# Windowed attention feeding a two-layer FFN: 128-token units for the first groups, a staged fp32 first block, 64-row score matmuls, and DMA transposes from the second batch on

## The chip, the core and the metric

One core of one Trainium2 chip runs the whole program. The metric is device time in microseconds (us), the median of several executions; fast executions of one kernel agree here within about 1%. A profile is one of these executions, recorded by the hardware. Its span runs from the first to the last instruction; it is some 2 us shorter than the time of the run.

## The reference

There are 8 batches, 8 heads, 576 tokens and a head size of 64. Attention looks back over at most 128 tokens, with a linear bias per head. Its output, read as 4608 tokens of 512 features, goes through two matrix products with a squared ReLU between them.

```python
scores = q @ k.T / 8                          # per batch and head, 576 x 576
rel    = pos[:, None] - pos[None, :]
scores = where((rel >= 0) & (rel < 128), scores - slope[h] * abs(rel), -1e9)
x      = softmax(scores) @ v                  # then 4608 tokens x 512
out    = relu(x @ w_in) ** 2 @ w_out          # w_in 512 x 2048, w_out 2048 x 512
```

All inputs and the output are fp32 in device memory.

## The kernel before

A small planner in Python lists every piece of work with an estimated duration, simulates the engines, and emits the instructions of each engine in the order that came out. On the chip each engine then as a rule takes its list in that order. If the next item's data is not there, the engine waits, even if a later item could run.

Attention is cut into 40 blocks of up to 128 tokens: five per batch, 128, 128, 128, 128 and 64 tokens. Blocks are numbered here from 0 through all batches, so block 5 is the first of the second batch. The FFN is cut into nine groups of 512 tokens. The pieces that matter:

```python
# loads: all by GpSimd's software queue, fp32 -> bf16 on the way
nc.gpsimd.dma_start(o, src[b, :, kb*128:kb*128+n, :].rearrange("h s d -> s h d"))   # k, q, v of one block
# order of loads: blocks 0-4, w_in (4 quarters), blocks 5-9, w_out (4 quarters), the rest

# per block: q and k transposed on TensorE (8 per block), copied out; q into tiles half zero
nc.tensor.transpose(slot.tile[:, i*128:(i+1)*128], src[:, (i % C)*128:(i % C + 1)*128], ident)

# scores of two heads at once: 128 rows, the zeros of qp keep the heads apart, 2n columns
nc.tensor.matmul(ps[:, :, part, 0:n], kT[...][:, c, :], qp[...][:, c, :, 0:n], start=True, stop=True)
...                                            # exp (ScalarE), mask (VectorE), P @ v, normalise
nc.tensor.transpose(xp[:, c*128:(c+1)*128], xt[...][:, c*128:(c+1)*128], ident)     # 4 per block

# FFN, group g: 16 steps of 4 matmuls with 512 columns (h), then 16 parts of 4 matmuls (o)
nc.tensor.matmul(h, w_in_sb[:, cc, fc*128:(fc+1)*128], xT[:, cc, g*512:(g+1)*512], ...)
nc.tensor.matmul(o, g_tile[:, fc, t*128:(t+1)*128], w_out_sb[:, fc, :], ...)
```

Group 0 cannot start before all of blocks 0 to 3 are in `xT`.

The softmax here doesn't subtract the row's maximum and nothing guards it: scores larger than these inputs give would overflow.

Of the kernel before, what the change touches and what calls it, by code (L numbers as in the profile page):

```python
# [14 lines left out]
class Task:  # L15


    __slots__ = ("engs", "key", "emit", "deps", "acq", "rel", "nout", "users",
                 "ready", "start", "end", "eng", "seq", "lat", "dma")

    def __init__(self, engs, key, emit, deps=(), acq=(), rel=(), lat=None, dma=None):

        self.engs, self.key, self.emit = engs, key, emit
        self.deps = [d for d in deps if d is not None]
        self.acq, self.rel, self.lat = list(acq), list(rel), lat
        self.dma = dma
        self.users, self.ready, self.start, self.end = [], 0.0, None, None
# [9 lines left out]
class Plan:  # L37


    LAT = {"PE": 260.0, "ACT": 220.0, "DVE": 220.0, "POOL": 200.0, "SP": 2200.0}  # L40
    BEGIN = {"POOL": 1250.0}
# [14 lines left out]
    def order(self):  # L56
        used = {tag: [] for tag in self.bufs}
        free = {}
        cand = {}
        left = {}  # L60
        for t in self.tasks:
            left[t] = len(t.deps)
            for d in t.deps:
                d.users.append(t)
            for e in t.engs:
                free.setdefault(e, self.BEGIN.get(e, 800.0))
                cand.setdefault(e, [])
# [5 lines left out]
        def avail(t):  # L73
            at = t.ready
            for s in t.acq:
                u = used[s.tag]
                n = self.bufs[s.tag]
                if len(u) >= n:
                    old = u[len(u) - n]
                    if old.left:  # L80
                        return None
                    at = max(at, old.freed)
            return at
# [3 lines left out]
        while len(done) < n_all:  # L87
            best = None
            for e, c in cand.items():
                lo = None  # L90
                for t in c:
                    a = avail(t)
                    if a is None:
                        continue
                    st = max(a, free[e])
                    k = (st, t.key, t.seq)
                    if lo is None or k < lo[0]:
                        lo = (k, t)
                if lo is not None and (best is None or lo[0][0] < best[0]):
                    best = (lo[0][0], e, lo[1])  # L100
            if best is None:
                raise RuntimeError("plan is stuck: " + repr([
                    (e, t.key, [s.tag for s in t.acq if avail(t) is None]) for e, c in cand.items() for t in c
                    if e != "POOL"][:40]))
            st, e, t = best
            t.eng, t.start = e, st
            dur = t.engs[e]
            if t.dma is not None:
                at = max(st + dur + 900.0, self.dma_free)
                self.dma_free = at + t.dma  # L110
                t.end = self.dma_free + 900.0
# [23 lines left out]
def kernel(  # L135
# [16 lines left out]
    NBLK = B * NKB  # L152

# [7 lines left out]
    far = const.tile([128, 2, 128], FP32)  # L161
    w_in_sb = const.tile([128, C, d_ff], BF16)
# [3 lines left out]
    def ring(name, n, shape):  # L166
        return [const.tile(shape, BF16, name=f"{name}_{i}") for i in range(n)]



    size = {"kn": 4, "qn": 4, "v": 6, "kT": 4, "qp": 3, "P": 3, "x": 2}
    kn = ring("kn", size["kn"], [128, d_model])
    qn = ring("qn", size["qn"], [128, d_model])
    vt = ring("vt", size["v"], [128, H, D + 1])
    kT = ring("kT", size["kT"], [128, C, 128])
    qp = ring("qp", size["qp"], [128, C, 2, 128])
    Pt = ring("P", size["P"], [128, H, 2, 128])
    xt = ring("x", size["x"], [128, d_model])

    plan = Plan({"h": 2, "o": 2, "s": 2, "att": 2, "rec": 4, "rt": 3, "g": 2, "osb": 3, **size})  # L180

    def act(n):
        return n * 0.84 + 55.0
# [3 lines left out]

    def mm(n):
        return max(n, 64) / 2.4 + 1.5



# [4 lines left out]
    t_iota = plan.add({"POOL": 360.0}, -9e5 + 0.012, build_iota)  # L197
# [4 lines left out]
    t_ident = plan.add({"DVE": 230.0}, -9e5 - 1, build_ident, [t_iota])  # L202
# [8 lines left out]
    t_dist = plan.add({"DVE": 1300.0}, -9e5 + 0.5, build_dist, [t_ident])  # L211
    t_mask = []

    for h in range(H):
        def build_mask(h=h):
            nc.scalar.activation(masks[:, h], dist, AF.Exp, bias=0.0,  # L216
                                 scale=-(2.0 ** (-8.0 * (h + 1) / H)))
        t_mask.append(plan.add({"ACT": act(256)}, -9e5 + h, build_mask, [t_dist]))

    def zero():  # L220
        for t in qp:
            nc.vector.memset(t[0:64, :, 1, :], 0.0)
            nc.vector.memset(t[64:128, :, 0, :], 0.0)
    t_zero = plan.add({"DVE": 2000.0}, -9e5, zero)

    def ones():
        for t in vt:
            nc.vector.memset(t[:, :, D:D + 1], 1.0)
        for t in vt[NKB - 1:]:
            nc.vector.memset(t[64:128, :, 0:D], 0.0)  # L230
    t_ones = plan.add({"DVE": 1200.0}, -9e5 + 1, ones)


    def load(key, ns, emit, deps=(), acq=()):
        return plan.add({"POOL": 900.0}, key, emit, deps, acq, dma=ns)
# [4 lines left out]
    def load_w_in(key):  # L240
        for n in range(4):
            def emit(n=n):
                w = d_ff // 4
                nc.gpsimd.dma_start(
                    w_in_sb[:, :, n * w:(n + 1) * w],
                    moe_w_in[:, n * w:(n + 1) * w].rearrange("(c p) f -> p c f", p=128))
            t_win[n] = load(key + n, 2550.0, emit)

    def load_w_out(key):
        for n in range(4):  # L250
            def emit(n=n):
                nc.gpsimd.dma_start(
                    w_out_sb[:, 4 * n:4 * n + 4, :],
                    moe_w_out[n * 512:(n + 1) * 512, :].rearrange("(c p) f -> p c f", p=128))
            t_wout[n] = load(key + n, 2550.0, emit)

    s_in, t_in = {}, {}

    def load_block(m, key):
        b, kb = divmod(m, NKB)  # L260
        n = blk[kb]
        for i, (nm, dst, src, tag) in enumerate((("k", kn, k, "kn"), ("q", qn, q, "qn"), ("v", vt, v, "v"))):
            sl = s_in[m, nm] = Slot(tag)

            def emit(dst=dst, src=src, sl=sl, nm=nm):
                o = dst[sl.idx]
                o = o[0:n, :, 0:D] if nm == "v" else o[0:n].rearrange("s (h d) -> s h d", h=H)
                nc.gpsimd.dma_start(o, src[b, :, kb * 128:kb * 128 + n, :].rearrange("h s d -> s h d"))  # L268
            t_in[m, nm] = load(key + 0.01 * i, 1050.0 * n / 128, emit, [t_ones] if nm == "v" else [], [sl])

    for m in range(NKB):
        load_block(m, -9e5 + m)
    load_w_in(-8e5)
    for m in range(NKB, 2 * NKB):
        load_block(m, -7e5 + m)
    load_w_out(-6e5)
    for m in range(2 * NKB, NBLK):
        load_block(m, -5e5 + m)


    t_xT = {}
    chain = {"tp": [], "s": [], "pv": [], "xp": []}

    def copy(task, o, i):
        if task.eng == "DVE":
            nc.vector.tensor_copy(o, i)  # L286
        else:
            nc.scalar.activation(o, i, AF.Copy)  # L288

    def attention(m):  # L290
        b, kb = divmod(m, NKB)
        n = blk[kb]
        due = (b * S + kb * 128 + n) / 4 - 192 - 150
        first = b == 0


        sk, sq = Slot("kT"), Slot("qp")
        sk_of[m] = sk
        slot = Slot("h" if first else "att")
        last = None  # L300
        for i in range(2 * C):
            def emit(i=i):
                nm = "kq"[i // C]
                src = (kn if i < C else qn)[s_in[m, nm].idx]
                if i == 0:
                    slot.tile = psum.tile([128, 1024], BF16, tag=slot.tag, name="tp")
                nc.tensor.transpose(slot.tile[:, i * 128:(i + 1) * 128], src[:, (i % C) * 128:(i % C + 1) * 128],  # L307
                                    ident)
            last = plan.add({"PE": mm(128)}, due - 56, emit,
                            [last, t_ident, t_in[m, "kq"[i // C]]] + ([t_in[m, "q"]] + chain["tp"] if i == 0 else []),  # L310
                            [slot, sk, sq] if i == 0 else [], [s_in[m, "kq"[i // C]]] if i % C == C - 1 else [])
        chain["tp"] = [last]

        def evac_k():
            copy(t_k, kT[sk.idx][:, :, 0:n], slot.tile[:, 0:512].rearrange("p (c s) -> p c s", c=C)[:, :, 0:n])
        both = {"ACT": act(C * n), "DVE": dve(C * n, 2)}
        t_k = plan.add(both if first else {"DVE": both["DVE"]}, due - 56, evac_k, [last], [], [slot])
        t_q = []
        for c2 in range(2):
            def evac_q(c2=c2):  # L320
                po = c2 * 64
                o = qp[sq.idx][po:po + 64, :, c2, 0:n]
# [182 lines left out]
    key = 0  # L505
# [46 lines left out]
```

## Time and profile before

The time before is 350.76 us (4 runs, 350.66 to 350.84). The page of the profile, its first two parts (busy us and share of the span; then busy tenths in 40 slices of 8.7 us):

```profile
span 349.0 us, 6481 instructions
PE 329.7 (94%) x2451; PEld 186.9 (54%) x2496; DVE 198.2 (57%) x600; ACT 203.2 (58%) x392; POOL 107.3 (31%) x133
PE   2689999999999999999999999999999999999995
DMA  9999999999999579595796867760000100110021
```

TensorE (PE) is busy almost throughout, and the DMA row stands at 9 for the first 113 us; I call that "full". (The row adds up the times of packets, which overlap, so that the sum per engine can come to more than 1.) "Busy" is pipelined time: neighbouring matmuls overlap, so it does not tell what a matmul costs. For that, read the starts. Lines of the timeline of TensorE around 145 us (start, duration, operation, count):

```profile
143.14 0.19 PE L382 MATMUL pv<-vt_83,P_94 128*128 128x65 bf16 x1
143.17 0.20 PE L382 MATMUL pv<-vt_84,P_94 128*128 128x65 bf16 x1
145.14 0.39 PE L307 MATMUL tp<-ident,kn_72 128*128 128x128 bf16 x4
145.37 0.39 PE L307 MATMUL tp<-ident,qn_76 128*128 128x128 bf16 x4
145.59 1.03 PE L483 MATMUL o<-w_out_sb,g 128*128 128x512 bf16 x3
```

The P·V matmul of 65 columns lasts 0.19 us, but the next starts 0.03 us later. Eight transposes go by in 0.45 us, so one costs 56 ns. In the same way 512 columns cost 215.7 ns and 256 columns 109 ns. Multiplying by the counts gives the table below. I call the rest of the span *lost time*: the time up to some moment, less the start-to-start cost of the matmuls begun by then. (Some h and o matmul records are missing from the traces, so these two kinds were counted by their weight loads, which are complete.)

| TensorE work before | count | us |
|---|---|---|
| h and o, 512 columns | 1152 | 248.5 |
| scores, 256 or 128 columns | 224 + 64 | 28.0 |
| P·V, 65 columns | 576 | 17.0 |
| transposes of k, q and x | 480 | 26.7 |
| sum | | 320.2 |
| lost before the last matmul | | 24.6 |
| last evacuation and store | | 4.2 |

Most of the loss comes early: 20.1 of the 24.6 us are lost by 40 us. The chain that ended last shows the moment when the first FFN matmul could start (start us, us, what):

```profile
27.56 0.32 DVE xT L286
27.89 0.04 issue
27.93 0.38 PE h L454
```

Only attention of the first batch ran until 27.9 us.

### The profile page before, as it was taken

Reading aid. Unit: us, or ns where it says so; the run is one execution under the profiler, and the core shown is the slowest. Engines: PE = TensorE matmul, PEld = TensorE weight load, DVE = VectorE, ACT = ScalarE, POOL = GpSimd, SP = SyncE. Lnnn points to the kernel's source line nnn. Section 1 sums busy time; section 2 is a strip of 40 time slices with the busy share of each in tenths; the row PEclk is TensorE's granted clock in tenths of the full one; section 3 lists DMA queues with packets and bytes.
Section 4 is the critical chain, followed back from the end, with each engine's and each line's share of the span. In section 5 each row is a group of like instructions: output and inputs, shape, how many; then the busy total and the mean of one; then the engine's idle time right before and its main releaser. Section 6 shows DMA issues by size and latency. Waiting matters only on the chain.

```text
span 349.0 us, 6481 instructions
## 1 busy us (share of the span) xinstructions
PE 329.7 (94%) x2451; PEld 186.9 (54%) x2496; DVE 198.2 (57%) x600; ACT 203.2 (58%) x392; POOL 107.3 (31%) x133
## 2 busy tenths in 40 slices
PE   2689999999999999999999999999999999999995
PEld 1565565576655555555555555555555444444442
DVE  6676796688876666656666566756666222222200
ACT  4585884886865666656665666755665344444411
POOL 8956747565534235232334234110000000000000
PEclk9999999999999999999999999999999999999999
DMA  9999999999999579595796867760000100110021
GB/s 76 141 198 162 165 192 154 87 118 74 123 102 85 62 76 92 62 84 62 73 92 67 78 68 73 73 68 31 30 15 33 48 30 32 38 52 32 30 84 66
DMA packets 121951, 28.20 MB, mean 81 GB/s; under 512 B 113217, under 2 KB 117313, under 8 KB 121921
## 3 DMA queue, kind: packets, MB, share of 16 engines
q0 software_dynamic: 116736, 18.36, 72.0%
q1 hardware_dynamic: 5184, 9.44, 7.3%
q8 instruction: 19, 0.31, 0.4%
q14 instruction: 12, 0.09, 0.1%
HBM read 36.70 MB, written 9.44 MB: 132 GB/s over the span
## 4 chain that ended last, share of the span: by engine, by line
PE 87%; DVE 6%; ACT 5%; issue 1%; ACTq 0%
PE o L483 34%; PE h L454 33%; PE ps_s L341 8%; PE tp L307 5%; PE pv L382 4%; PE xp L421 2%; ACT qp_90 L288 1%; DVE P_92 L367 1%; ACT masks L216 1%; ACT qp_91 L288 1%; ACT rt L462 1%; DVE x_96 L408 0%; ACT P_93 L359 0%; DVE qp_91 L286 0%; ACT P_92 L359 0%
## 5 line engine op out<-in xcount | busy, mean ns | idle before, releaser
L454 PE MATMUL h<-xT,w_in_sb 128*128 128x512 bf16 x557 | 158.7, 379 | 1.0
L483 PE MATMUL o<-w_out_sb,g 128*128 128x512 bf16 x550 | 150.2, 379 | 1.3
L462 ACT ACTIVATE rt<-h 128x512 bf16<-128x512 f32 x144 | 85.5, 596 | 66.2 <-PE h L454 62.4
L468 DVE TENSOR_TENSOR g<-rt 128x512 bf16<-128x512 bf16 x144 | 60.4, 420 | 62.0 <-ACT rt L462 59.9
L483 PEld LDWEIGHTS <-g 128*128 128x128 bf16 x576 | 54.1, 98 | 51.2
L454 PEld LDWEIGHTS <-w_in_sb 128*128 128x128 bf16 x576 | 54.3, 98 | 44.3 <-issue 0.2
L359 ACT ACTIVATE P_92<-ps_s 128x512 bf16<-128x512 f32 (+1 forms) x56 | 27.3, 506 | 12.2 <-PE ps_s L341 11.9
L494 ACT ACTIVATE osb<-o 128x512 f32<-128x512 f32 x36 | 21.5, 597 | 19.1 <-PE o L483 18.8
L359 ACT ACTIVATE P_94<-ps_s 128x512 bf16<-128x512 f32 (+1 forms) x52 | 26.0, 517 | 10.2 <-PE ps_s L341 9.8
L359 ACT ACTIVATE P_93<-ps_s 128x512 bf16<-128x512 f32 (+1 forms) x52 | 26.0, 517 | 9.7 <-PE ps_s L341 9.2
L367 DVE TENSOR_TENSOR P_92<-P_92,masks 128x512 bf16<-128x512 bf16 (+1 forms) x56 | 20.0, 363 | 8.6 <-ACT P_92 L359 8.2
L403 DVE RECIPROCAL rec<-pv 128x4 f32<-128x4 f32 (+1 forms) x80 | 14.0, 176 | 16.3 <-PE pv L382 15.8
L367 DVE TENSOR_TENSOR P_93<-P_93,masks 128x512 bf16<-128x512 bf16 (+1 forms) x52 | 19.0, 369 | 7.1 <-ACT P_93 L359 6.5
L367 DVE TENSOR_TENSOR P_94<-P_94,masks 128x512 bf16<-128x512 bf16 (+1 forms) x52 | 18.9, 368 | 6.2 <-ACT P_94 L359 5.8
L286 DVE COPY xT<-xp 128x512 bf16<-128x512 bf16 (+1 forms) x39 | 15.3, 393 | 8.5 <-PE xp L421 8.4
L408 DVE TENSOR_TENSOR x_95<-pv,rec 128x256 bf16<-128x256 f32 (+1 forms) x40 | 16.8, 419 | 0.7
L408 DVE TENSOR_TENSOR x_96<-pv,rec 128x256 bf16<-128x256 f32 (+1 forms) x40 | 16.6, 418 | 0.6
L268 POOL DMA_DIRECT2D kn_74<-in_k_dram x10 | 8.5, 845 | 19.7 <-PE tp L307 11.5
L382 PEld LDWEIGHTS <-P_92 128*128 128x128 bf16 x200 | 10.2, 99 | 6.0 <-DVE qp_90 L286 0.7
L268 POOL DMA_DIRECT2D kn_71<-in_k_dram x10 | 8.6, 863 | 14.2 <-PE tp L307 12.1
L268 POOL DMA_DIRECT2D kn_73<-in_k_dram x10 | 8.6, 862 | 13.2 <-PE tp L307 12.1
L382 PEld LDWEIGHTS <-P_93 128*128 128x128 bf16 x192 | 9.8, 101 | 4.7 <-DVE P_93 L367 0.3
(101 smaller groups left out, 403.5 us busy)
## 6 DMA issues: line engine op xcount, KB each, us to landing
out_dram<-osb SPq DMA_DIRECT2D x36, 256.0 KB, 2.0
w_in_sb<-in_moe_w_in_dram POOLq DMA_DIRECT2D x4, 512.0 KB, 10.2
w_out_sb<-in_moe_w_out_dram POOLq DMA_DIRECT2D x4, 512.0 KB, 9.9
kn_71<-in_k_dram POOLq DMA_DIRECT2D x8, 128.0 KB, 3.4
qn_75<-in_q_dram POOLq DMA_DIRECT2D x8, 128.0 KB, 4.4
kn_72<-in_k_dram POOLq DMA_DIRECT2D x8, 128.0 KB, 4.3
qn_76<-in_q_dram POOLq DMA_DIRECT2D x8, 128.0 KB, 4.2
kn_73<-in_k_dram POOLq DMA_DIRECT2D x8, 128.0 KB, 4.3
```

What stands on the lines that cost most here:

```text
L268: nc.gpsimd.dma_start(o, src[b, :, kb * 128:kb * 128 + n, :].rearrange("h s d -> s h d"))
L307: nc.tensor.transpose(slot.tile[:, i * 128:(i + 1) * 128], src[:, (i % C) * 128:(i % C + 1) * 128], ident)
L341: nc.tensor.matmul(slot_s.tile.rearrange("p (c t q) -> p c t q", c=2, t=2)[:, :, part, 0:n], kT[sk_of[mk].idx][:, c, :], qp[sq.idx][:, c, ...
L359: nc.scalar.activation(view(Pt[sP.idx][:, 2 * c:2 * c + 2]), view(slot_s.tile.rearrange("p (c t q) -> p c t q", c=2, t=2)), AF.Exp, bias=0 ...
L367: nc.vector.tensor_tensor(pt, pt, view(masks[:, 2 * c:2 * c + 2]), op=ALU.mult)
L382: nc.tensor.matmul(slot_v.tile[:, hi * (D + 1):(hi + 1) * (D + 1)], Pt[sP.idx][:, h, part, :], vt[s_in[mk, "v"].idx][:, h, :], start=part ...
L408: nc.vector.tensor_tensor(xt[sx.idx][0:n, hf * 256:(hf + 1) * 256].rearrange("p (h e) -> p h e", h=4), pv[0:n, :, 0:D], srec.tile[0:n, :]. ...
L454: nc.tensor.matmul(slot.tile, w_in_sb[:, cc, fc * 128:(fc + 1) * 128], xT[:, cc, g * 512:(g + 1) * 512], start=cc == 0, stop=cc == C - 1)
L462: nc.scalar.activation(srt.tile, slot.tile, AF.Relu, bias=0.0, scale=1.0)
L468: nc.vector.tensor_tensor(sg.tile[:, fc, :], srt.tile, srt.tile, op=ALU.mult)
L483: nc.tensor.matmul(slot.tile, sg.tile[:, fc, t * 128:(t + 1) * 128], w_out_sb[:, fc, :], start=fc == 0, stop=fc == FCB - 1)
L494: nc.scalar.activation(so.tile, slot.tile, AF.Copy)
```

## The change

The intent was to take the k, q and x transposes off TensorE, to replace the half-empty score matmuls by pairs on 64 rows each, and to let the FFN begin after one block instead of four. The diff is long because the planner was reworked too. Its core:

```diff
+    N_HW = 1          # blocks loaded fp32 on the hardware queues (SP, ACT), cast on VectorE
+    N_PE = 5          # blocks transposed on TensorE; from block 5 on by DMA
+    N_WARM = 6        # matmuls on zeros at the start
+    LEAD = 60         # how far ahead of its use a block is ordered, in keys (4 per work item)
-    size = {"kn": 4, "qn": 4, "v": 6, "kT": 4, "qp": 3, "P": 3, "x": 2}
+    size = {"kq": 4, "v": 7, "kqT": 4, "P": 3, "x": 3}
...
+    first = ["b0", "b1", "i0", "i1", "b2", "i2", "i3", "b3", "b4", "b5", "o0", "o1", "b6", "o2", "o3"]
...
+        if on_pe:                     # m < N_PE: 8 transposes on TensorE as before
+        else:
+                nc.sync.dma_start_transpose(out=kqT[sT.idx][:, :, 0:n], in_=kq[s_kq[m].idx][0:n, :])
+            t_f = plan.add({"SP": 1700.0 * n / 128}, due - 60, flip, t_kq[m], [sT], [s_kq[m]],
+                           dma=1000.0 * n / 128, name=f"kqT{m}")
...
-                    nc.tensor.matmul(... kT[...][:, c, :], qp[sq.idx][:, c, :, 0:n], start=True, stop=True)
+            for grp in range(2):
+                for j in range(2):
+                    c = 2 * grp + j
+                    for part, mk in parts:
+                        for r in range(2):          # two heads: rows 0-63 and rows 64-127, two PSUM banks
+                            rows = slice(64 * r, 64 * r + 64)
+                            nc.tensor.matmul(o, kT[mk][rows, c, :], kT[m][rows, C + c, 0:n], start=True, stop=True)
...
+                nc.sync.dma_start_transpose(out=xT[:, :, t0:t0 + n], in_=xt[sx.idx][0:n, :])
...
+    work_list = [("unit", 0, r, qd) for r in range(4) for qd in range(4)]   # 128 tokens x a quarter of d_ff
+    for u in range(16):
+        work_list += [("unit", 1, u // 4, u % 4), ("o", 0, u // 4, u % 4)]
```

Note the load order: w_out now comes before most of the second batch. All DMA transposes and all stores share the sync engine's queue (SP).

## The prediction

> **What bounds the kernel now.** TensorE. The page puts matmul busy at 94% of a 349.0 us span, but that is pipelined time, so I count start-to-start intervals in the timeline: 215.7 ns for a 512-column matmul, 109 for 256 columns, 56 for 128, 30 for the 65-column P·V ones. That gives 248.5 us for the 1152 matmuls of the two weight products, 28 for scores, 17 for P·V, 27 for the 480 transposes of q, k and x: about 320 us. The window from 140 to 180 us, counted so, comes to 40.0 us: TensorE is full. Only about 29 us are not work: some 19 lost before the first weight-product matmul at 27.9 us (until then only batch 0's attention runs, half of it at 107 ns spacing), some 6 of stalls between 28 and 100 us, and 3.8 at the end (last evacuation and store). VectorE (57%) and ScalarE (58%) do not bound.
>
> **What the change does, on TensorE.**
> - The PE transposes of 35 of 40 blocks go: 35 x 12 x 56 ns = 23.5 us, from the full stretch, so all critical. They become DMA transposes on the sync queue: latency, with a lead of about 15 work items.
> - Scores: no zero half, 64-row matmuls in pairs. The Trainium skill ("TensorE: Matmul & The Clock Gate", Part 3) says that matmuls in different row groups run concurrently; no trace here shows it yet. Estimate: a pair cannot beat two of the 30 ns steps of P·V, so 8 pairs take 0.48 us against 0.87 now; but "TensorEngine Tiling (Array Packing)", Key Properties, says that changing tiling mode drains the array, perhaps 0.2 to 0.3 us per burst. Short blocks lose. Net gain 1 to 4 us, not 14. If pairs don't overlap, 5 to 9 us are lost.
> - Units of 128 tokens in groups 0 and 1: 512 matmuls at 56 ns instead of 128 at 216: +1 us.
> TensorE work then: about 296 us.
>
> **Start.** First unit at 11 to 13 us instead of 27.9. But loads now set the pace: a weight quarter takes about 2.7 us of the DMA, a block about 3 (issues and landings). Batch 0, w_in, w_out and blocks 5 to 8 come in until about 50 us, so units wait for the third and fourth quarters (near 20 to 23 us), and output parts for w_out (near 33). I expect 12 to 15 us lost here, plus 3 to 6 of later stalls. The fp32 first block gains about 1 us of landing.
>
> **Sum.** 296 + 14 + 4 = 314 us, range 303 to 328. Faster by over 2%: 0.94; within 2%: 0.04; slower: 0.02.
>
> **What would show it.** TensorE transposes fall from 480 to 60; first h matmul at 11 to 13 us, with waits for w_in and w_out; score matmuls start in near pairs, 0.45 to 0.55 us per full burst, with a gap of 0.1 to 0.2 us before and after; 100 us onward still full; VectorE and ScalarE busy fall by about 35 and 15 us; DMA transposes land 2 to 4 us after issue.
>
> **What would make it wrong.** DMA transposes slow or colliding with loads, so that xT comes late and TensorE waits in the middle; the sync queue, in order, holding stores behind waiting transposes; score pairs that don't overlap, or dearer drains; a colder TensorE in the sparse first 30 us; or loads faster than assumed, which would bring 303 or less.

## The result, and the profile after

The time after is 331.46 us (4 runs, 330.56 to 333.07). The ratio to before is 0.9458, 95% interval 0.9427 to 0.9489. Ratios are the mean time of one kernel's fast runs over that of the other's of the same rounds, so not quite the ratio of the medians quoted. The gain is 19 us; 37 were forecast, and 331.46 lies above the range.

The profiled run took 333.07 us, the slowest of the four, 1.6 us above their median. The lines of its page that answer to those shown of before:

```profile
span 331.3 us, 7042 instructions
PE 304.8 (92%) x2713; PEld 167.7 (51%) x2754; DVE 169.4 (51%) x509; ACT 166.9 (50%) x336; POOL 104.8 (32%) x130
PE   5889869888994999999999999979999999999995
DMA  9999999999999999999999959991996203100021
```

TensorE's work fell, but its row now has holes between 40 and 110 us (slices of 8.3 us). The DMA row stays full to about 190 us, where before it was full to 113 us. The chain that ended last names what TensorE waited for in the holes:

```profile
29.02 16.29 DMA w_out_sb<-in_moe_w_out_dram
55.66 6.06 DMA xT<-x
66.06 9.32 DMA xT<-x
98.07 5.61 DMA xT<-x
```

The last quarter of w_out took 16.3 us to land. Three transposes of x took 5.6 to 9.3 us each, and all four stand on the chain. TensorE's timeline at these places, with the idle time in brackets:

```profile
13.43 2.85 PE L551 MATMUL h<-xT,w_in_sb 128*128 128x128 bf16 x25
45.35 4.44 PE L592 MATMUL o<-w_out_sb,g 128*128 128x512 bf16 x12 [2.85 <-DMA w_out_sb<-in_moe_w_out_dram]
75.43 1.28 PE L551 MATMUL h<-xT,w_in_sb 128*128 128x128 bf16 x16 [1.80 <-DMA xT<-x]
103.73 0.61 PE L569 MATMUL h<-xT,w_in_sb 128*128 128x512 bf16 x1 [4.09 <-DMA xT<-x]
```

The FFN begins at 13.4 us, as intended, but at half rate: its first matmuls of 128 columns start 107 ns apart, not 56, and the clock record has 0.50 from 7.9 to 18.1 us. (The kernel before had these 107 ns steps too, until 21.1 us.) At 45.35 us twelve 512-column matmuls take 4.44 us where 12 x 0.216 = 2.6 us are usual. The reason is the granted clock, here over three stretches around that wait (us, busy us and count of matmuls, clock, DMA packet time per engine as a multiple of the stretch, GB/s):

```profile
41.00:45.40 4.40, 1.07 (x5) 1.00 1.59 134
45.40:48.80 3.40, 3.40 (x9) 0.50 2.34 151
48.80:52.20 3.40, 3.40 (x23) 0.99 2.23 196
```

After the idle stretch the clock was halved for 3.4 us. Two more such windows follow, at 76 and 103 us, behind waits of 1.8 and 4.1 us for xT. The Trainium skill ("TensorE: Matmul & The Clock Gate", Part 1) describes this: an idle window of about 3.4 us drops the array to half rate. The trace agrees in the length of the windows and differs in the condition: in the 3.4 us before each of the three drops TensorE was idle for 2.85, 1.80 and all 3.41 us, so a window that was idle for about half was enough. (It is not always: a 1.80 us wait at 220 us was followed by none.) Each of these three holes cost up to another 1.7 us.

The same account as before, for the profiled runs of both kernels. A change of tiling mode was measured at 0.215 us per score burst (shown below) and is listed apart.

| | before | after |
|---|---|---|
| TensorE work at the start-to-start costs | 320.2 | 284.2 |
| mode changes, 40 x 0.215 | 0 | 8.6 |
| lost by 40 us | 20.1 | 15.8 |
| lost from 40 to 110 us | 4.2 | 16.4 |
| lost from 110 us on | 0.3 | 2.1 |
| last evacuation and store | 4.2 | 4.2 |
| span | 349.0 | 331.3 |

So 27.4 us of TensorE work went and the start improved by 4.3 us, but 12.2 us came back between 40 and 110 us and 1.8 us later: 17.7 us in all.

### The profile page after: what moved, and what is told of

It reads as the page before. It is cut to its first block, busy times and chain, and to the rows that moved or that the text cites. A ratio compares the mean times of both kernels' runs of the same rounds, so it can differ in the third digit from the quotient of the medians.

```text
span 331.3 us, 7042 instructions
## 1 busy us (share of the span) xinstructions
PE 304.8 (92%) x2713; PEld 167.7 (51%) x2754; DVE 169.4 (51%) x509; ACT 166.9 (50%) x336; POOL 104.8 (32%) x130
## 4 chain that ended last, share of the span: by engine, by line
PE 80%; DMA 13%; DVE 2%; issue 2%; POOL 1%; ACT 1%; POOLq 0%
PE o L592 35%; PE h L569 30%; DMA xT<-x 6%; PE h L551 5%; DMA w_out_sb<-in_moe_w_out_dram 5%; PE s L398 5%; PE pv L441 5%; DMA kq<-in_q_dram 2%; POOL kq L310 1%; ACT P L414 1%; DVE x L462 1%; DVE P L427 0%; PE tp L364 0%; PE xp L474 0%; POOL vt L314 0%
## 5 line engine op out<-in xcount | busy, mean ns | idle before, releaser
L569 PE MATMUL h<-xT,w_in_sb 128*128 128x512 bf16 x437 | 110.7, 383 | 6.6 <-DMA xT<-x 4.1
L414 ACT ACTIVATE P<-s 128x512 bf16<-128x512 f32 (+1 forms) x160 | 69.9, 521 | 34.4 <-PE s L398 34.4
L427 DVE TENSOR_TENSOR P<-P,masks 128x512 bf16<-128x512 bf16 (+1 forms) x160 | 57.0, 368 | 21.4 <-ACT P L414 17.6
L310 POOL DMA_DIRECT2D kq<-in_k_dram x39 | 33.3, 853 | 92.5 <-DMA kqT<-kq 86.9
L314 POOL DMA_DIRECT2D vt<-in_v_dram x39 | 33.2, 852 | 41.5 <-PE pv L441 34.3
L551 PE MATMUL h<-xT,w_in_sb 128*128 128x128 bf16 x512 | 34.6, 229 | 3.7 <-DMA xT<-x 2.8
L310 POOL DMA_DIRECT2D kq<-in_q_dram x39 | 33.2, 852 | 6.0 <-DMA w_out_sb<-in_moe_w_out_dram 2.9
L551 PEld LDWEIGHTS <-w_in_sb 128*128 128x128 bf16 x512 | 31.6, 103 | 4.9 <-issue 2.3
L462 DVE TENSOR_TENSOR x<-pv,rec 128x256 bf16<-128x256 f32 (+1 forms) x80 | 32.2, 415 | 0.7
L441 PEld LDWEIGHTS <-P 128*128 128x128 bf16 x576 | 25.6, 99 | 13.0 <-DVE P L427 1.8
L441 PE MATMUL pv<-vt,P 128*128 128x65 bf16 x576 | 28.2, 195 | 1.4 <-DVE P L427 1.2
L207 ACT ACTIVATE osb<-o 128x512 f32<-128x512 f32 x19 | 11.4, 599 | 13.7 <-PE o L592 12.9
```

The source lines that it names most:

```text
L310: nc.gpsimd.dma_start(o, source(src, m))
L314: nc.gpsimd.dma_start(vt[s_v[m].idx][0:n, :, 0:D], source(v, m))
L414: nc.scalar.activation(view(Pt[sP.idx], w), sS[i].tile.rearrange("p (j t q) -> p j t q", j=2, t=2)[:, :, p0:2, 0:n], AF.Exp, bias=0.0, sca ...
L427: nc.vector.tensor_tensor(pt, pt, view(masks, w), op=ALU.mult)
L441: nc.tensor.matmul(sv.tile[:, hi * (D + 1):(hi + 1) * (D + 1)], Pt[sP.idx][:, place(h), part, :], vt[s_v[mk].idx][:, h, 0:D + 1], start=pa ...
L462: nc.vector.tensor_tensor(xt[sx.idx][0:n, hf * 256:(hf + 1) * 256].rearrange("p (h e) -> p h e", h=4), heads(sv)[0:n, :, 0:D], sr.tile[0:n ...
```

## The experiments

Two theories were put against each other. **Theory A**: the DMA engines are full in the first 110 us, and a DMA transpose takes engine time from the loads of w_out and of the next blocks. The Trainium skill ("DMA: Bandwidth & Descriptors", Issuing engines are not separate DMA queues) says that DMAs of all issuing engines run on the same 16 DMA engines and interleave; experiment 13 agrees, with 15.1 us of delay. **Theory B**: DMA rate is not short; the planned order is. TensorE's list was made with a transpose landing sooner than it does, so TensorE stands before an item whose data is late.

All edits are to the kernel after. The lost times are by the account above, mode changes included, so the kernel after stands at 43.0 us. The queue lines of the page for both kernels are the starting point (packets, MB, share of 16 engines' span):

```profile
q0 software_dynamic: 116736, 18.36, 72.0%
q1 hardware_dynamic: 5184, 9.44, 7.3%
```

```profile
q0 software_dynamic: 113616, 17.96, 79.7%
q1 hardware_dynamic: 57888, 22.36, 37.0%
kqT<-kq SPq DMA_TRANSPOSE x35, 5.1
xT<-x SPq DMA_TRANSPOSE x35, 5.0
```

Before (first fence), the hardware queue carried the stores only. After (second fence), it carries 53,000 more packets, nearly half as many as all loads, and the packets of the loads take a larger share of a shorter span. A transpose lands 5 us after its issue, in the median.

### 1. No DMA transposes

```diff
-    N_PE = 5
+    N_PE = 40
-        attention(m, need[m] - LEAD if m >= N_PE else -1e5 + 200 * m)
+        attention(m, need[m] - LEAD if m >= 5 else -1e5 + 200 * m)
```

> All 40 blocks transposed on TensorE again (no DMA transpose at all), the order of the attention blocks kept. TensorE work rises by 35 x 12 x 56 ns = 23.5 us, to about 308. Theory A (the DMA transposes take engine time from the loads of the first 110 us): the four w_out quarters land 2.6 to 2.8 us apart instead of the 3.8 us of the last three after the change, the last one near 40 instead of 45.3 us; the lost time falls from 43 to about 30 us; total 342 to 346. Theory B (TensorE takes its instructions in an order planned with wrong latencies; DMA rate is not short): w_out lands where it did (44 to 46), lost time still falls as xT no longer comes by DMA, total about the same 340 to 346. So the w_out landings decide, the total does not.

Measured: 344.37 us, ratio to before 0.9824 [0.9804, 0.9844]. The two landing lines of w_out tell the theories apart (us from issue to landing, minimum, median, maximum), first of the kernel after, then of this one:

```profile
DMA to landing us min/median/max: 6.6/11.4/16.3
```

```profile
DMA to landing us min/median/max: 6.6/10.2/12.9
```

Without transposes the last two quarters land 2.5 us apart instead of 3.9, and the last one at 42.3 instead of 45.3 us. That speaks for A. TensorE work rose by 22.7 us and lost time fell from 43.0 to 31.6 us. So the DMA transposes as placed took some 23 us off TensorE and gave 11 back.

### 2. DMA transposes from the third batch on

```diff
-    N_PE = 5
+    N_PE = 10          # and the order of blocks kept, as in 1
```

> The second batch's five blocks are transposed on TensorE too, DMA transposes only from the third batch. TensorE work +3 us. Theory A: no transpose is in flight while w_out is loaded, so w_out lands about 5 us earlier and the stalls between 40 and 110 us (18 us of lost time) fall by 6 to 12: total 323 to 328. Theory B: these blocks don't depend on DMA latency any more, but later ones do as before; the w_out stall stays (6 us of lost time between 39 and 48); total 328 to 332.

Measured: 325.66 us, ratio 0.9297 [0.9276, 0.9318], 5.8 us faster than the kernel after. Lost time fell by 11 us, as much as in experiment 1, at a price of 3.1 us of TensorE work. (The spans of the two profiled runs differ by 8.1 us, the medians by 5.8, as the kernel after was profiled in its slowest run.) Most of the harm was therefore done by the second batch's transposes. (Not all of it: experiment 5 takes another 5 us off by correcting the order of the later ones.) The w_out quarters land as without any transpose (the last at 42.9 us). Of the gain, 3.3 us come before 60 us and the larger part between 60 and 110 us.

### 3. Only the planner's latency corrected

```diff
-                t.end = self.dma_free + self.LAND
+                t.end = self.dma_free + self.LAND + t.late      # late=3500.0 on kqT and x, else 0
```

> Only the planned order changes: the planner is told that DMA transposes land 3.5 us later than it thought, near what the trace shows (median 5 us). Same instructions, same transfers. Theory A: within 1% of 331.5, since the loads are no faster. Theory B: TensorE does other ready work in place of waiting, lost time falls by 5 us or more, 326 or less.

Measured: 328.21 us, ratio 0.9367 [0.9343, 0.9392]. A 3.3 us gain lies between the two expectations. The w_out wait stays (4.3 us of idle, and the same 45.5 us landing); the waits for xT fall from 6.9 to 0.2 us of idle, and lost time by 4.3 us. Order is thus a part of the loss, but not all of it.

### 4. w_out ahead of blocks 5 and 6

```diff
-    first = [..., "b3", "b4", "b5", "o0", "o1", "b6", "o2", "o3"]
+    first = [..., "b3", "b4", "o0", "o1", "o2", "o3", "b5", "b6"]
```

> Only the load order changes: the four w_out quarters before blocks 5 and 6. w_out should land by about 39 us in place of 45.3, so the 6 us lost between 39 and 48 us go. Theory A: the loads are the limit, so blocks 5 and 6 come 5 to 10 us later and the wait reappears as a wait for xT; total within 1% of 331.5. Theory B: the stall was only order, and about 5 us are gained, 326.

Measured: 332.48 us, ratio 0.9496 [0.9471, 0.952]. w_out landed at 36.3 us and the hole at 40 to 48 us went. Lost time at 50 us was 16.3 us instead of 23.2. At 70 us it was 29.3 instead of 25.0: the wait came back as a 6.6 us wait for xT. A shortage that moves when the order of loads changes fits a shortage of DMA, as A says.

### 5. and 6. Corrections 2 and 3 together, and a longer lead

> Both changes that helped together: second batch transposed on TensorE, and the planner told that DMA transposes land 3.5 us later. If the two repair different losses (engine time early, order later), the gains add in part: 325.7 less 1 to 3 us, 322.5 to 324.5. If both repaired the same stall, 325 to 326.5.

> Second batch on TensorE, and attention blocks ordered 120 keys (30 work items) ahead of their use in place of 60. Theory B (order too tight for the real latency): the remaining waits for xT after 90 us go, 321 to 324. Theory A (loads short): no more than 1 us from 325.7, as the rings of four, not the keys, bound how far ahead a block can be.

Measured: 320.53 us, ratio 0.9146 [0.9122, 0.917], for the two corrections together; 321.76 us, ratio 0.9195 [0.9164, 0.9226], for experiment 2 with `LEAD = 120` and no correction of the latency. The corrections add up, with a little more gain than forecast, and a longer lead does nearly the same as a truthful latency. That A allowed the lead no more than 1 us was wrong: 3.9 us came.

### 7. Neighbouring score matmuls on the same 64 rows

```diff
-                for j in range(2):
-                    c = 2 * grp + j
-                    for part, mk in parts:
-                        for r in range(2):
+                for r in range(2):
+                    for j in range(2):
+                        c = 2 * grp + j
+                        for part, mk in parts:
```

> Same 576 score matmuls of 64 rows, but ordered so that neighbours use the same 64 rows. If neighbours on different rows run together (the trace: two starts per 56 ns), a full burst grows from about 0.41 to 0.86 us from first to last start, TensorE work by 24 x 0.45 + 8 x 0.23 + 8 x 0.24 = 14.6 us, total 341 to 346. If the pairs did not overlap, nothing changes.

Measured: 331.79 us, ratio 0.9469 [0.943, 0.9508]: no change, and the expectation missed. It does not mean that pairs don't overlap. The starts of one burst of the kernel after, and then of this one (names with two tiles are matmuls of the earlier key block, part 0; those with one tile are of part 1):

```profile
178.00 0.23 PE L398 MATMUL s<-kqT,kqT 64*128 64x128 bf16 x2
178.07 0.22 PE L398 MATMUL s<-kqT 64*128 64x128 bf16 x2
178.40 0.22 PE L398 MATMUL s<-kqT 64*128 64x128 bf16 x2
178.55 1.04 PE L569 MATMUL h<-xT,w_in_sb 128*128 128x512 bf16 x4
```

```profile
177.48 0.24 PE L398 MATMUL s<-kqT,kqT 64*128 64x128 bf16 x2
177.54 0.23 PE L398 MATMUL s<-kqT 64*128 64x128 bf16 x2
177.60 0.23 PE L398 MATMUL s<-kqT,kqT 64*128 64x128 bf16 x2
```

In both, two matmuls start per 56 ns. In the kernel after, the two starts of a pair are some 3.5 ns apart. The Trainium skill ("TensorE: Matmul & The Clock Gate", Part 3) gives about 4 ns between the starts of such neighbours, and the trace agrees. In the experiment the program order is part 0, part 1, part 0, part 1 on one half of the rows, then the same on the other half, yet the trace has two starts of part 0 followed by two of part 1. The two halves seem to have drawn from the list at the same time, offset by 13 to 19 ns. So this edit did not separate the pairs and says nothing of what pairs are worth. Experiment 8 does.

### 8. Score matmuls over all 128 rows

```diff
-                            rows = slice(64 * r, 64 * r + 64)
+                            rows = slice(0, 128)
```

> Wrong result on purpose: the same 576 score matmuls contract all 128 rows (two heads summed), so no change of tiling mode and no pairs. By the trace a full burst costs 0.65 us with the gaps at its two ends; 16 x 56 ns are 0.89 us. Sum over 24 full, 8 first and 8 short blocks: 5.8 + 0.2 + 0.3 = 6.3 us more TensorE work; as TensorE is full after 110 us, about 4 to 6 us of it show: 335 to 338. The gaps of 0.10 and 0.12 us around a burst vanish. If the gaps don't come from the mode change they stay and the total is nearer 340.

Measured: 335.99 us, ratio 0.9577 [0.956, 0.9594], 4.5 us slower than the kernel after. (The comparison with the reference passed all the same: q and k are a tenth of a normal draw, so summing two heads' scores changes little.) A burst and its neighbour:

```profile
177.51 0.28 PE L398 MATMUL s<-kqT,kqT 128*128 128x128 bf16 x2
177.63 0.28 PE L398 MATMUL s<-kqT 128*128 128x128 bf16 x2
178.30 0.28 PE L398 MATMUL s<-kqT 128*128 128x128 bf16 x2
178.41 1.03 PE L569 MATMUL h<-xT,w_in_sb 128*128 128x512 bf16 x4
```

Sixteen matmuls of 128 rows take 0.90 us. The gap before the burst (median over all bursts 0.096 us in the kernel after) and the one behind it (0.120 us) are both zero here. These gaps are the price of going to 64 rows and back: 0.215 us per burst, 8.6 us over 40 blocks. The Trainium skill ("TensorEngine Tiling (Array Packing)", Key Properties) says that changing the tiling mode drains the array; this trace agrees and puts a number to it. With its gaps, a full burst costs 0.65 us against 0.87 before the change, so the score part of the change is worth 24 x 0.223 us for the full blocks and almost nothing for the other 16, or about 5.5 us in all.

### 9. A shallower ring of loaded blocks

```diff
-    size = {"kq": 4, "v": 7, "kqT": 4, "P": 3, "x": 3}
+    size = {"kq": 2, "v": 7, "kqT": 4, "P": 3, "x": 3}
```

> Ring of loaded k and q blocks from 4 to 2, nothing else: loads run two blocks less ahead. Theory A in its sharper form (loads far ahead of need crowd out transposes that are needed now: at 98 us block 20 was being loaded while TensorE waited for block 12): median landing of a transpose falls from 5 us below 4, the waits for xT after 60 us shrink, total 326 to 330. Against it: with less run-ahead the early loads wait for ring places and the total rises, 333 to 338.

Measured: 336.52 us, ratio 0.9593 [0.9551, 0.9635]. Transposes landed little faster (medians 4.8 and 4.4 us) and the total rose. The idea that loads running far ahead crowd out the transposes found no support: less run-ahead was worse. (The edit does not isolate it, as the smaller ring also delays the early loads.)

### 10. and 11. The other two parts undone, one each

```diff
-    work_list = [("unit", 0, r, qd) for r in range(4) for qd in range(4)]
+    work_list = [("fc", 0, u) for u in range(16)]          # 10: group 0 in 512-token steps
```
```diff
-    N_HW = 1
+    N_HW = 0                                               # 11: block 0 by the software queue
```

> Group 0 again in steps of 512 tokens (group 1 keeps its units). The first h matmul then waits for block 3's xT, near 32 us in place of 13.4 us. Between those times the units did about 9 us of work. If the early start is worth what it shows, the total rises by 6 to 9 us, 337 to 341. If the loads of w_out and of the second batch set the pace until 50 us anyway, the moved work fills the hole at 39 to 48 us and the total rises by at most 3 us, 331 to 334.5.

> The first block is loaded by the software queue with the cast, like the others; no casts on VectorE. The first transpose waits till 4.8 us (k) and 6.3 us (q) as in the kernel before, in place of 5.2 us, so block 0 is about 1 us later; every later load moves 2 to 3 us later in issue, though the DMA engines, full from 2 us on, move less data (the staged block is written in fp32). Expected: within 1% of 331.5, at most 3 us slower.

Measured: 333.4 us, ratio 0.9494 [0.9447, 0.9541], without the units of group 0; 335.4 us, ratio 0.9558 [0.9534, 0.9581], without the hardware-queue load. Group 0 then began at 32.9 us instead of 13.4, and the median rose by only 2 us, which is not clear of noise (the interval overlaps that of the kernel after, 0.9427 to 0.9489). The work moved into holes that were there anyway. The hardware-queue load, forecast as at most 3 us, is worth 3.9. The landings suggest why: with block 0 on GpSimd's queue every later load moves, w_in's last quarter from 21.8 to 25.0 us and w_out's from 45.3 to 48.7 us. Both results fit the view that DMA sets the pace of the first 50 us.

### 12. The best of the corrections with a longer lead

> Second batch on TensorE, planner told of 3.5 us later transposes, and 120 keys of lead. If what is left after 110 us in the version at 320.5 us is still order, 318.5 to 320; if not, 320 to 322.

Measured: 320.11 us, ratio 0.9138 [0.9109, 0.9167]. The longer lead adds 0.4 us to the 320.53 us version, which is no more than the runs of one kernel differ.

### 13. Six spare transposes that nobody reads

Experiments 1 to 4 change the order, the waits and the DMA load at once. This one puts in DMA load alone, on top of the 320.53 us version (the edit shortened).

```diff
+            if m in (2, 3):
+                for i in range(3):
+                    nc.sync.dma_start_transpose(out=scratch[3 * (m - 2) + i], in_=kqT[sT.idx]...)
```

> The version at 320.5 us (second batch on TensorE, planner told) plus six DMA transposes of 128 x 1024 that nobody reads, between about 20 and 40 us, with nothing waiting for them and TensorE's order unchanged. Theory A (a transpose costs the loads engine time): w_out's last quarter, which landed near 42 us, lands 4 to 9 us later, and the total rises by 3 to 8 us, 323.5 to 328.5. Theory B (only the latency of transposes that are waited for, and the order): no change, below 321.5.

Measured: 336.57 us (median of the 3 fast runs; 337.62 with the slow one), ratio 0.9612 [0.9578, 0.9646]. TensorE executes the same list as in the 320.53 us version (all 2814 weight loads in the same order), and the profile shows no instruction that waits for these transposes. The landing lines of w_out, first of the 320.53 us version, then of this one:

```profile
L268 POOL DMA_DIRECT2D w_out_sb<-in_moe_w_out_dram x4: 750/778/797, 24.5 to 29.3; - x4
DMA to landing us min/median/max: 6.6/9.9/12.6
```

```profile
L269 POOL DMA_DIRECT2D w_out_sb<-in_moe_w_out_dram x4: 740/748/761, 27.0 to 39.5; - x4
DMA to landing us min/median/max: 17.3/17.9/20.4
scratch<-kqT SPq DMA_TRANSPOSE x6, 12.9
```

The last quarter was issued at 39.5 us and landed 17.5 us later, at 57.0 us, instead of at 41.9. Six transposes of 256 KB put 15.1 us of loads back, 2.5 us each. The three loads of a whole block take as long (in the kernel after, those of block 2 landed at 14.6, 15.4 and 16.2 us, directly behind a w_in quarter at 13.7). Lost time at 60 us rose from 19.4 to 33.3 us. This shows A directly. The cost, 16 us in all, was even above my range. In the kernel after two transposes of the second batch were in flight before w_out's last quarter landed (27.4 to 37.6 and 38.2 to 47.2 us), and w_out came 3.0 us later than without any, which fits.

### 14. Only blocks 5 to 7 moved back to TensorE

```diff
-    N_PE = 5
+    N_PE = 8           # order of blocks kept as in 1, planner told as in 3
```

> As the version at 320.5 us, but only blocks 5, 6 and 7 (not 8 and 9) are moved back to TensorE: 24 transposes or 1.3 us less TensorE work. If the harm is done before 60 us, by the transposes of blocks 5 to 7 beside w_out, 319 to 320.5; if blocks 8 and 9 matter too, 321 to 324.

Measured: **318.61 us**, ratio to before 0.9093 [0.9078, 0.9108], correct, the fastest kernel. It beats both kernels, the one after by 12.9 us. Its TensorE and clock rows of the page:

```profile
PE   5789899999999999999999999999999999999995
PEclk9999999999999999999999999999999999999999
```

The holes of 40 to 110 us are gone, and with them their cold windows. Lost time at 110 us is 21.2 us, against 35.5 in the kernel after, for 2.0 us more TensorE work. (The clock row does not speak for the start: the clock records of this profile begin at 17.5 us, and the row shows 9 before them, while matmuls of 128 columns started 107 ns apart until then.)

## Why the prediction was wrong, point by point

The direction was right, and the gain was half of what was forecast. The predicted sum was 296 + 14 + 4 = 314 us; the terms as measured (profiled run, 333.07 us):

| term | predicted | measured |
|---|---|---|
| TensorE work with mode changes | 296 | 292.8 |
| lost at the start (to 40 us) | 14 | 15.8 |
| later stalls | 4 | 18.5 |
| last evacuation and store | left out | 4.2 |
| run time beyond the span | left out | 1.8 |

- **The step that failed** is "They become DMA transposes on the sync queue: latency, with a lead of about 15 work items", and with it "plus 3 to 6 of later stalls". The later stalls came to 18.5 us. A DMA transpose is not only latency: on full DMA engines it displaces loads. Experiment 13 shows about 2.5 us of displaced loads for each large one. In the kernel after, the transposes of the second batch fell in the stretch where w_out and that batch were being loaded. The prediction named "DMA transposes slow or colliding with loads" among the risks but put no time on it, though the page it had read shows the DMA row at 9 there. The kernel's planner has the same term too small: it charges a q and k transpose 1.0 us of DMA time (`dma=1000.0` in the diff). A plan with 2.5 us was not run.
- **Order added to it.** Telling the planner the latency alone gained 3.3 us on the kernel after (experiment 3). Both repairs together, with three batch-two blocks on TensorE, gave 12.9 us (experiment 14). How much of the 16.4 us lost between 40 and 110 us belongs to displaced loads and how much to order cannot be split exactly, because each repair also shortens the other's waits. Each cold window after one of the three holes adds up to 1.7 us.
- **The sum left two terms out.** The account of the kernel before had 3.8 us for the end, yet the sum has no such term, nor one for the 1.7 us between the span and the time of the run. With both, the same reasoning would have said about 320 us. That is still a miss of 11 us, so this slip is the smaller part.
- **The TensorE term was right**, 3 us too high. The transposes fell as counted, to 60. The drain of 0.2 to 0.3 us per burst was measured at 0.215. The pairs gain about 5.5 us net where 1 to 4 were forecast, because a full burst costs 0.65 us with its gaps, not some 0.73.
- **The start was right in time but not in worth.** The first h matmul came at 13.4 us (11 to 13 forecast), and 15.8 us were lost by 40 us (12 to 15 forecast). But the units that make the early start possible are worth only some 2 us for group 0, not clear of noise (experiment 10); that DMA sets the pace behind them is the likely reason. The fp32 first block, forecast at 1 us of landing, is worth 3.9 us; by the landings, because everything behind it on GpSimd's queue comes some 3 us earlier. The risk of a colder TensorE at the start came true (clock 0.50 from 7.9 to 18.1 us), but the kernel before was no warmer there.
- **Landings were underestimated**: 5 us in the median, where 2 to 4 were forecast, and up to 10.2 us in the busy stretch.
- VectorE and ScalarE busy time fell by 29 and 36 us, where about 35 and 15 were forecast. Neither bounds.

Open: why a DMA transpose displaces so much. The queue lines of the pages give a hint: with the six spare transposes q1 has 56,992 packets, without them 50,656, so a transpose of 256 KB goes as some 1,050 packets of about 250 bytes. Whether the cost goes by packets was not tested. Also open is a 1.8 us wait of TensorE at 220 us in the kernel after for which the profile names no cause; it is not in the later versions.

## What to carry to other kernels

Work that is moved from a full engine to the DMA engines is not free while those are full: before counting it as latency, look at the DMA row of the page where the new transfers will fall, and charge each its engine time against the loads it sits beside. A row of 9s is a warning and no proof: it stood at 9 to 190 us in the kernel after, while only 2.1 us were lost after 110. Start such a move after the load rush; three blocks fewer on DMA were worth 9.6 us here (328.21 to 318.61, the planner told in both). Where an engine follows a fixed list, give the planner measured landings, and end a prediction with an account that adds up to the whole run time, tail and launch included.

## What the Trainium skill lacked or had wrong

- "DMA: Bandwidth & Descriptors" (Latency and other measured facts) gives a DMA transpose 261 GB/s in a non-contiguous and some 350 to 400 GB/s in a contiguous case, and "Advanced Engine Details and Errata" (X-Bar Transpose) calls it as fast as a regular DMA. Beside software-queue loads on full engines, each 128 x 1024 bf16 transpose from SBUF to SBUF set the loads back by 2.5 us (15.1 us for six), or about 104 GB/s of its 256 KB (a delay of other transfers, so not quite the same measure as a rate). That the queues share the engines is on the first page, and the runs agree; what a transpose costs the others is on none.
- "TensorE: Matmul & The Clock Gate" (Part 3) says that matmuls start and end in program order, never reordered. In experiment 7 the starts of 64-row matmuls on different halves of the rows interleaved against the program order, two starts per 56 ns, as if each half had a list of its own. This is read from tile names and starts of the records, not from a direct test.
- "TensorEngine Tiling (Array Packing)" (Key Properties) says that a mode change drains the array but gives no cost: 0.096 us before and 0.120 us behind a burst here, zero without the change.
- "TensorE: Matmul & The Clock Gate" (Part 1) says that the array drops to half rate after at least one idle window of about 3.4 us. The length agrees (3.41 us at clock 0.50), but two of the three drops in the kernel after followed windows in which TensorE was idle for only 2.85 and 1.80 us. The page also warns that clock records can be unreliable. Here they were only incomplete: in the kernel before they begin at 21.07 us, which is where matmuls of 128 columns go from 107 to 56 ns apart, while the profile's clock row shows 9 for the time before.
